# The last sequence's up products as seven block products (Strassen's identity) in an attention and gated-product kernel

## Chip, cores and metric

The kernel runs on one core of a Trainium2 chip. The metric is the device time of one execution in microseconds (us), the median of several runs. Engine names in profile rows: PE is TensorE (PEld its weight loads), DVE is VectorE, ACT is ScalarE, POOL is GpSimd, SP is the engine whose queue issues nearly all DMAs.

## What is computed

```python
def _attn_ref(q, k, v):                 # 4 sequences, 8 heads, 768 tokens, 64 wide
    k_sum = k.reshape(B, H, nb, 32, D).max(axis=3)
    v_sum = v.reshape(B, H, nb, 32, D).mean(axis=3)
    scores_l = scale * q @ k.T          # only where |i - j| < 16
    scores_s = scale * q @ k_sum.T + log(32)
    a = softmax(concatenate([scores_l (masked), scores_s]))
    return a @ concatenate([v, v_sum])

x = attn_out.transpose(0, 2, 1, 3).reshape(3072, 512)
a = x @ w_a                             # 512 x 1536
b = x @ w_b                             # 512 x 1536
return (a * b) @ w_out                  # 1536 x 512
```

## The kernel before

**Precision.** Every large operand is split into a high and a low part that together hold it in float32. A product of two such operands is three matmuls: high by high, high by low, low by high. The float64 weights are brought in as pairs of 32-bit words, joined and split once (`convert`, L451 on), and then stay in SBUF. `weight(f, nm)` is the tile of one block f of 128 of the 1536 columns, nm being a, b or o (w_out).

**Stages.** The tokens are worked in chunks u: the first sequence in three chunks of two tiles of 128 tokens, each further sequence in two chunks of three tiles. Chunks 7 and 8 are the last sequence. An item (u, f) (`item`, L1172) makes, for a chunk of three tiles:
- the up products a and b (`up`, L1151): for each, 4 blocks of the 512 inputs x 3 parts = 12 matmuls of 128x384 into PSUM banks h0 and h1;
- the gate: ACT copies a into g (L1255), DVE multiplies b by g in PSUM (L1258), ACT casts the product to the high part gh (L1260), DVE subtracts for the low part gl (L1263);
- the down products (L1273): for each tile three matmuls of 128x512, summed over the 12 blocks f in banks o0 to o2. After the last f the banks are copied to S1 and stored.

The gate of one item runs while the next item's a is on TensorE. The very last item keeps banks of its own, and its last tile is stored in two halves (L1302 to L1326).

**Attention** of one tile of 128 queries (`scores`, `transposes`, `products`): 16 small matmuls of scores into banks c0 and c1 (L734); for each half of the heads DVE scales and masks (L759) and takes the maximum (L767), ACT makes four exponentials with their sums (L781) and adds 1e-9 (L797), DVE takes the reciprocal (L801), POOL divides (L816); DVE transposes twelve 32x32 patterns over all eight heads (L862, 256 elements per partition); the value products, 16 or 32 small matmuls (L882), go to bank o3. For all tiles but the last of a sequence they are split over two banks: ACT copies one (L904), DVE adds (L907). Then `split` casts the high part (L911) and subtracts for the low part (L915), which are the operands of `up`. The value burst of a tile and the score burst of the next are always issued together. Keys are transposed and their maxima taken once per sequence (L627 to L648); means of values are summed by POOL (L665).

**What sets the order.** Every operation is added to a planner (`Work`) with an engine, a rank, an estimate of its time, and keys that it reads and writes. `emit` picks, engine by engine, the ready operation with the lowest rank; the tables in `ORDER` fix the order by operation number up to about chunk 3. After that the estimates and ranks decide. All engines and SP's queue run what is emitted in order. In the main loop `next(rest)` adds the next tile of attention at chosen items: a chunk's attention is added during the chunk before it, so that attention of chunk 8 runs beside the products of chunk 7.

Of the kernel before, what the change touches and what calls it, by code (L numbers as in the profile page):

```python
# [9 lines left out]
F32 = mybir.dt.float32  # L10
# [20 lines left out]
        547 549 545 558 554 559 555-557 568 564 566 588 567 565 573 585 593 574 594 846 847 854  # L31
        852 853 699 861 859 860 868 866 755 867 873-875 882 880 881 889 809 887 735 888 896 903
        894 895 910 901 902 789 908 909 952 915 917 924 916 843 922 923 929 930 986 987 994 992
        993 995 1002 1000 1001 1027 1028 1003 1066 1008 1009 1067 1074 1072 1073 1075 1082
# [16 lines left out]
        7 3 11 23 15 19 60 59 80 79 72 65 66 73 74 195 67 85-87 196 92 205 93 94 200 201 206 215  # L51
        125 126 216 155 131 156 132 133 138 117 147 139 161 210 162 140 163 236 211 168-170 451
# [6 lines left out]
        441 443 437 643 447 590 572 620 644 592 621 581 645 622 587 623 630 624 631-635 577 636  # L59
        849 637 646-648 851 649 650 856 858 700 702 701 703 754 597 863 716 709 865 870 734 872  # L60
# [3 lines left out]
        954 926 1026 955 845 928 956 962 933 989 969 991 974-982 997 983 984 999 985 1030 1033  # L64
        1034 1032 1005 1035 1036 1007 1106 1042 1049 1069 1054 1055 1071 1056-1064 1077 1065
        1079
# [5 lines left out]
        1229-1232 1234-1237 963 1835 970 1836 1837 1839 1238 1840-1842 1844-1847 1043 1050  # L72
        1849-1853 1856-1858
# [16 lines left out]
    """,  # L90
}

# [1328 lines left out]
```

## Time and profile before

| | us |
|---|---|
| three timed runs | 654.15, 654.19, 654.43 (median 654.19) |
| profiled execution, span from first to last instruction | 652.9 |
| busy: PE, DVE, ACT, POOL | 645.3, 405.3, 255.9, 112.6 |
| DMA | 54.75 MB, mean 84 GB/s |

The profile gives no time of its own for the profiled execution beside the span. The page has these parts: busy time of each engine (1), slices (2), DMA queues (3), the chain of work that ended last, followed back from the end (4), the costliest groups of instructions (5) and DMA issues (6). A matmul's recorded duration overlaps with the next one's; what it costs is seen in the chain in order of time, where a piece lasts until the next begins. PE works at 99% of the span; the other engines are mostly idle, and their idle time costs nothing as long as PE does not wait for them.

### The profile page before, as it was taken

The numbers are of one execution on the slowest core, as the hardware profiler recorded it, in microseconds if no ns is written. First come the engines' busy times: TensorE is split into PE (matmuls) and PEld (weight loads), VectorE is DVE, ScalarE is ACT, GpSimd is POOL, SyncE is SP. The second block draws the span as 40 slices with busy tenths as digits, with TensorE's granted clock in tenths as the row PEclk, the third lists the DMA queues.
The fourth block names the chain that finished last, engine by engine and source line by source line (L and its number), as shares of the span: only waits on it lengthen the run. The fifth ranks groups of instructions, "written<-read, shape, count | busy, mean of one in ns | idle before, by whom it ended". The sixth has DMA issues, their size and how long they took to land.

```text
span 652.9 us, 13600 instructions
## 1 busy us (share of the span) xinstructions
PE 645.3 (99%) x5327; PEld 598.5 (92%) x5327; DVE 405.3 (62%) x830; ACT 255.9 (39%) x750; POOL 112.6 (17%) x202
## 2 busy tenths in 40 slices
PE   8999999999999999999999999999999999999997
PEld 6898888899989999999999999999999999999997
DVE  3789999997785776476646578367456556122212
ACT  3996964523443441333423441144414334121111
POOL 6420030156433431011101100011001011000000
PEclk9999999999999999999999999999999999999999
DMA  9999954554433443421212113132101200010001
GB/s 214 257 230 291 345 141 112 118 122 107 131 80 91 99 96 60 98 49 18 41 27 66 35 34 63 26 94 42 28 14 26 73 10 15 1 49 1 0 1 49
DMA packets 158200, 54.75 MB, mean 84 GB/s; under 512 B 135736, under 2 KB 151352, under 8 KB 158136
## 3 DMA queue, kind: packets, MB, share of 16 engines
q1 hardware_dynamic: 157992, 53.75, 34.5%
q8 instruction: 42, 0.69, 0.4%
q14 instruction: 22, 0.18, 0.1%
q10 hardware_dynamic: 144, 0.13, 0.1%
HBM read 47.41 MB, written 6.44 MB: 82 GB/s over the span
## 4 chain that ended last, share of the span: by engine, by line
PE 95%; ACT 2%; SPq 1%; DMA 1%; issue 1%; DVE 0%; DVEq 0%
PE h L1151 57%; PE o L1273 29%; PE o L882 3%; PE c L734 3%; SPq L353 1%; DMA space<-in_q_dram 1%; PE o L829 1%; PE c L1151 1%; ACT s L781 0%; PE h L1026 0%; PE h L882 0%; PE c L882 0%; PE o L734 0%; PE c L1384 0%; ACT space L781 0%
## 5 line engine op out<-in xcount | busy, mean ns | idle before, releaser
L1151 PE MATMUL h<-x,w 128*128 128x384 f32 (+2 forms) x2064 | 388.3, 321 | 0.1
L1151 PEld LDWEIGHTS h<-x,w 128*128 128x128 f32 x2064 | 331.2, 190 | 10.2 <-issue 0.5
L1273 PE MATMUL o<-w,gh 128*128 128x512 f32 x534 | 131.3, 381 | 0.0
L1260 ACT CAST gh<-h 128x384 fp32r<-128x384 f32 x71 | 33.9, 477 | 207.5 <-DVE h L1258 206.8
L1258 DVE TENSOR_TENSOR h<-h,g 128x384 f32<-128x384 f32 x71 | 40.1, 565 | 115.2 <-PE h L1151 109.7
L862 DVE STREAM_TRANSPOSE pt<-s 32x256 f32<-32x256 f32 x228 | 99.3, 436 | 14.9 <-POOL s L816 10.3
L1273 PEld LDWEIGHTS o<-w,gh 128*128 128x128 f32 x534 | 98.0, 189 | 11.5 <-issue 0.5
L816 POOL TENSOR_TENSOR s<-s,nml 128x480 f32<-128x480 f32 x40 | 43.8, 1096 | 309.9 <-DVE nml L801 309.3
L1151 PE MATMUL h<-late,w 128*128 128x384 f32 x288 | 93.9, 326 | 0.0
L781 ACT ACTIVATE s<-s,nml 128x120 f32<-128x120 f32 x160 | 61.5, 386 | 17.2 <-DVE nml L767 17.1
L1273 PE MATMUL o<-w,gl 128*128 128x512 f32 x231 | 64.0, 384 | 0.0
L1151 PEld LDWEIGHTS h<-late,w 128*128 128x128 f32 x288 | 54.4, 189 | 0.9
L1255 ACT COPY g<-h 128x384 f32<-128x384 f32 x71 | 33.9, 478 | 52.5 <-PE h L1151 52.5
L1263 DVE TENSOR_TENSOR gl<-h,gh 128x384 fp32r<-128x384 f32 x71 | 39.2, 552 | 21.2 <-ACT gh L1260 20.5
L1273 PEld LDWEIGHTS o<-w,gl 128*128 128x128 f32 x231 | 42.9, 189 | 7.2 <-issue 1.6
L665 POOL TENSOR_TENSOR S<-S 96x256 f32<-96x256 f32 (+3 forms) x58 | 33.1, 572 | 45.7 <-DMA S<-in_v_dram 36.3
L781 ACT ACTIVATION_READ_ACCUMULATOR s<-s,nml 128x1 f32 x160 | 30.1, 188 | 0.0
L907 DVE TENSOR_TENSOR o<-o,s 128x512 f32<-128x512 f32 x12 | 8.4, 700 | 32.4 <-ACT s L904 32.2
L759 DVE SCALAR_TENSOR_TENSOR s<-c,mask 128x480 f32<-128x480 f32 x40 | 26.2, 656 | 0.6 <-PE c L734 0.5
L767 DVE TENSOR_REDUCE nml<-s 128x4 f32<-128x480 f32 x40 | 26.1, 653 | 0.7
L1273 PE MATMUL o<-w,x 128*128 128x512 f32 x96 | 25.8, 385 | 0.0
L882 PEld LDWEIGHTS o<-pt,vw 64*64 64x64 f32 (+1 forms) x608 | 19.4, 136 | 5.6 <-issue 5.4
(147 smaller groups left out, 565.7 us busy)
## 6 DMA issues: line engine op xcount, KB each, us to landing
raw<-in_moe_w_a_dram SPq DMA_DIRECT2D x12, 512.0 KB, 6.8
raw<-in_moe_w_out_dram SPq DMA_DIRECT2D x12, 512.0 KB, 6.8
raw<-in_moe_w_b_dram SPq DMA_DIRECT2D x12, 512.0 KB, 7.9
out_dram<-S SPq DMA_DIRECT2D x23, 256.0 KB, 2.2
qin<-in_q_dram SPq DMA_DIRECT2D x288, 16.0 KB, 1.8
S<-in_v_dram SPq DMA_DIRECT2D x24, 192.0 KB, 2.8
kin<-in_k_dram SPq DMA_DIRECT2D x38, 100.0 KB, 2.5
vw<-in_v_dram SPq DMA_DIRECT2D x18, 192.0 KB, 3.2
```

The costliest lines, as they stand in the source:

```text
L665: lambda: nc.gpsimd.tensor_tensor(out=out, in0=i0, in1=i1, op=ALU.add),
L759: lambda h=h: nc.vector.scalar_tensor_tensor(out=s[h], in0=y[h], scalar=0.125, in1=mask[:, kind, None, :KN].broadcast_to([P, NP, KN]), op0 ...
L781: lambda h=h, c=c, sums=sums: nc.scalar.activation(s[h][:, c, :], x[h][:, c, :], AF.Exp, bias=m[:, 0, h, c : c + 1], scale=1.0, accum_out= ...
L816: lambda h=h, r=r: nc.gpsimd.tensor_tensor(out=s[h], in0=s[h], in1=r[:, :, None].broadcast_to([P, NP, KN]), op=ALU.mult,),
L862: lambda js=js, qs=qs, rs=rs: nc.vector.transpose(out=pv[js, rs, qs], in_=sv[qs, rs, js]),
L882: nc.tensor.matmul(bank[dst].rearrange("p (c x) -> p c x", x=P)[h * D : (h + 1) * D, c, es], vw[e][ks_, 2 * c + h, :], d[ks_, h, c, es], s ...
L1151: nc.tensor.matmul(ps, w[:, c, part, :], (xt[:, 4 * xpart : 4 * xpart + 4] if both else inputs_of(u, xpart))[:, :, c].rearrange("p g (a b) ...
L1255: act(CHAIN, 0.13 + W / 1030, [ak], gk, lambda: nc.scalar.copy(out=g, in_=pa))
L1258: lambda: nc.vector.tensor_tensor(out=pb, in0=pb, in1=g, op=ALU.mult),
L1260: act(CHAIN, 0.16 + W / 1030, [bk], [ghk], lambda: nc.scalar.copy(out=gh, in_=pb))
L1263: lambda: nc.vector.tensor_tensor(out=gl, in0=pb, in1=gh.bitcast(F32), op=ALU.subtract),
L1273: nc.tensor.matmul(bank[ok[j]], (gh if first else gl)[:, j * P : (j + 1) * P], w[:, :, part, :].rearrange("p (z a) n -> p z n a", a=2), st ...
```

## The change

**Seven products.** For the last sequence (chunks 7 and 8 together, `whole`) the operands are cut in two: the tokens into halves A1 and A2 (three tiles each), the 512 inputs into halves of 256, and the 256 output columns of one f into a and b. Up products a and b of both halves are then eight block products, each of six matmuls of 128x384. The Winograd form of Strassen's identity makes them from seven products of sums of blocks. With S1 = A21 + A22, S2 = S1 - A11, S3 = A11 - A21, S4 = A12 - S2 and T1 to T4 the like sums of weight blocks: P1 = A11 B11, P2 = A12 B21, P3 = S4 B22, P4 = A22 T4, P5 = S1 T1, P6 = S2 T2, P7 = S3 T3. Their outputs are added on DVE (`sum_`, from PSUM) and POOL (`sum_sb`, in SBUF), five sums on DVE, two on POOL and two gates of 384 columns per f (`step`).

**Sums of weights.** `mixtures(f)` makes T1 to T4 on POOL in float32 from the split weights (2 sums of 128x512, 4 of 128x256), splits them (ACT cast, POOL subtraction, 4 each) and stores them in DRAM (`comb`), with the three plain blocks that are needed, seven stores of 256 KB for each f. They are added at the items of `MIX`, in chunks 3 to 6, outside of the numbered order (`work.aside`). In the last stage `fetch` brings the seven blocks of each f back into a ring of eight places.

**Attention ahead, unrounded.** Chunk 6's products are needed at once and those of the last sequence before `whole`, so attention of chunks 6 to 8 runs earlier (`PLACES`: chunks 3 to 6 hold what 3 to 7 held). From chunk 6 on the result is kept in float32 (`kept`): chunk 6 and 7 through DRAM (`rawd`), chunk 8 in SBUF; the high and low parts are made later (`bring_back`, `inputs_`). The value products of these tiles go to one bank. From chunk 5 on each transposition is cut in two, over four heads each (`SPLIT`). The means of values of the last sequence are summed one sequence earlier.

**Down.** Tiles 0 to 3 of the six are summed over f in o0 to o3 as before. The gated parts of tiles 4 and 5 are kept in SBUF for all f, and their down products run at the end, tile 5 in two halves of 256 columns. Index shifts in `ORDER` and the removed special case of the last item are left out below.

```diff
+    WHOLE, RAW, SPLIT = NU - 2, NU - 3, 5
+    HT = 3 * P
...
+    comb = [dram.tile([8, P, 512], F32, tag=f"comb{f}", name=f"comb{f}") for f in range(NF)]
+    rawd = dram.tile([3 * WIDE, P, 512], F32, tag="raw", name="rawd")
...
-        halves = [slice(0, 4), slice(4, 8)] if False else [slice(0, 8)]
+        halves = [slice(0, 4), slice(4, 8)] if u >= SPLIT else [slice(0, 8)]
...
+        if u >= RAW:
+            other = None
...
-        return dk[0] + dk[1] + vk, [bk] + [other] * bool(other), fn, split
+        return dk[0] + dk[1] + vk, [bk] + [other] * bool(other), fn, kept if u >= RAW else split
...
-    items += [(0, NF - 1), (1, NF - 1)] + [(u, f) for u in range(2, NU) for f in range(NF)]
+    items += [(0, NF - 1), (1, NF - 1)] + [(u, f) for u in range(2, WHOLE) for f in range(NF)]
...
+    PLACES = {(3, 3): 1, (3, 6): 1, (4, 3): 1, (4, 6): 1, (4, 9): 1, (5, 0): 3, (6, 2): 9}
+    MIXED = [(3, 1), (3, 4), (4, 0), (4, 2), (4, 4), (4, 6), (5, 0), (5, 2), (5, 4), (6, 0), (6, 2), (6, 4)]
...
+    def mixtures(f):
...
+        for i, nm in enumerate("ab"):
+            pool(
+                60, 1.3, weight_key(f, nm), [RK[i], f"go{f}"],
+                lambda i=i, nm=nm: nc.gpsimd.tensor_tensor(
+                    out=r[i].rearrange("p h c x -> p (h c) x"), in0=weight(f, nm)[:, :, 0].bitcast(F32),
+                    in1=weight(f, nm)[:, :, 1].bitcast(F32), op=ALU.add,
+                ),
+            )
...
+            act(59, 0.36, [RK[i]], key, lambda: nc.scalar.copy(out=w(0), in_=x()))
+            pool(
+                59, 0.72, [RK[i]], key,
+                lambda: nc.gpsimd.tensor_tensor(
+                    out=w(1), in0=x(), in1=w(0).bitcast(F32), op=ALU.subtract
+                ),
+            )
+            move(
+                99.5, 262.0, 400, key, [f"comb{f}.{op}"], lambda: comb[f][op],
+                lambda: own().bitcast(F32),
+            )
...
+        PROD = {
+            1: ("first", 0, B11), 5: ("s1", 0, T1), 6: ("s2", 0, T2), 3: ("s4", 0, B22),
+            2: ("first", 2, B21), 7: ("s3", 0, T3), 4: ("a22", 0, T4),
+        }
+        TURN = {1: 0.0, 5: 0.1, 6: 0.3, 3: 0.4, 2: 0.5, 7: 0.6, 4: 1.2}
+        FETCH = (1, 5, 6, 3, 2, 7, 4)
+        def bank_of(n, k):
+            return ("h0", "h1", "c0", "c1")[(7 * n + FETCH.index(k)) % 4]
...
+        def step(n):
+            bk = {k: bank_of(n, k) for k in PROD}
+            fetch(n)
+            product(n, 1)
+            copy(bk[1], "p1")
+            product(n, 5)
+            copy(bk[5], "p5")
+            product(n, 6)
+            sum_("u2", bk[6], "p1")
+            sum_sb("c12", "u2", "p5")
+            product(n, 3)
+            sum_("c12", bk[3], "c12")
+            product(n, 2)
+            sum_(None, bk[2], "p1")
+            gate(n, 0, bk[2], "c12")
+            product(n, 7)
+            sum_("u3", bk[7], "u2")
+            sum_sb("c22", "u3", "p5")
+            product(n, 4)
+            sum_(None, bk[4], "u3")
+            gate(n, 1, bk[4], "c22")
...
-        if u is not None and FILL < u < NU - 1 and f in ((3, 7, 11) if u % 2 == 0 else (3, 6)):
-            next(rest)
+        for _ in range(PLACES.get((u, f), 0)):
+            next(rest, None)
+        if (u, f) == (5, 1):
+            bring_back()
+        if u is not None and u > FILL:
+            work.aside = True
+            for g in MIX.get((u, f), ()):
+                mixtures(g)
+            work.aside = False
```

**TensorE in the last stage.** Names: h_77, h_78, c_79, c_80 are the banks h0, h1, c0, c1; o_73 to o_76 are o0 to o3; w_ and gW_ behind the arrow are tiles in the place of former weights. Before, two items of chunk 8 (L1151 is up, L1273 down):

```order
L1151 MATMUL h_78<-x,w_1001 128x384 x12
L1151 MATMUL h_77<-x,w_1031 128x384 x12
L1273 MATMUL o_73<-w_1031,gh 128x512 x2
L1273 MATMUL o_74<-w_1031,gh 128x512 x2
L1273 MATMUL o_75<-w_1031,gh 128x512 x2
L1273 MATMUL o_73<-w_1031,gl 128x512
L1273 MATMUL o_74<-w_1031,gl 128x512
L1273 MATMUL o_75<-w_1031,gl 128x512
L1151 MATMUL h_78<-x,w_1052 128x384 x12
```

Now the middle of a step (L1527 is a product, L1639 a down matmul): three down matmuls of tile 3, P5, P4 of the step before, P6 (its six rows differ in the part of S2), down matmuls of tiles 0 and 1.

```order
L1639 MATMUL o_76<-w_762,w_1300 128x512 x3
L1527 MATMUL h_78<-w_728,w_1181 128x384 x6
L1527 MATMUL c_80<-w_1014,w_1065 128x384 x6
L1527 MATMUL c_79<-w_762,w_1181 128x384
L1527 MATMUL c_79<-w_899,w_1181 128x384
L1527 MATMUL c_79<-w_762,w_1181 128x384 x2
L1527 MATMUL c_79<-w_899,w_1181 128x384
L1527 MATMUL c_79<-w_762,w_1181 128x384
L1639 MATMUL o_73<-w_899,gW_0_6202 128x512 x3
L1639 MATMUL o_74<-w_899,gW_0_6202 128x512 x2
```

A step then goes on with P2, P3, four down matmuls, P7, P1 of the next step and three down matmuls. The four banks go round: each product takes the bank of the fourth product before it in the order 1, 5, 6, 3, 2, 7, 4.

**VectorE in one tile of attention.** Before, a tile of the last sequence, from the query transposition (L1095) over reciprocals (L801) and transpositions (L862) to the second gate product (L1258, with L1263 the low part):

```order
L1095 STREAM_TRANSPOSE qT<-qin 128x512
L1263 TENSOR_TENSOR gl<-h_78,gh 128x384
L801 RECIPROCAL nml_171<-nml_171 128x4 x2
L862 STREAM_TRANSPOSE pt<-s 32x8x32
L1258 TENSOR_TENSOR h_78<-h_78,g 128x384
L862 STREAM_TRANSPOSE pt<-s 32x8x32 x2
L1263 TENSOR_TENSOR gl<-h_78,gh 128x384
L862 STREAM_TRANSPOSE pt<-s 32x8x32 x9
```

Now the last tile of the last sequence (L765 and L773 scale and take maxima, L1278 and L1283 are the gate product and the low part, L807 the reciprocal, L868 a half transposition):

```order
L765 SCALAR_TENSOR_TENSOR s<-c_80,mask 128x4x120
L1278 TENSOR_TENSOR h_78<-h_78,g 128x384
L773 TENSOR_REDUCE nml_172<-s 128x4
L1283 TENSOR_TENSOR gl<-h_78,gh 128x384
L807 RECIPROCAL nml_172<-nml_172 128x4
L868 STREAM_TRANSPOSE pt<-s 32x4x32 x3
L807 RECIPROCAL nml_172<-nml_172 128x4
L868 STREAM_TRANSPOSE pt<-s 32x4x32 x5
L1278 TENSOR_TENSOR h_78<-h_78,g 128x384
L868 STREAM_TRANSPOSE pt<-s 32x4x32 x3
L1283 TENSOR_TENSOR gl<-h_78,gh 128x384
L868 STREAM_TRANSPOSE pt<-s 32x4x32 x13
```

The 24 half transpositions stand where 12 stood, and the first of them no longer stand behind the second half's division.

**POOL beside attention.** Before, the last sums of values (L665, L690) and key maxima (L568) come ahead of the third sequence's tiles, and then the divisions (L816), two for each tile, follow each other with nothing between:

```order
L665 TENSOR_TENSOR S_178<-S_178 96x64
L665 TENSOR_TENSOR vm<-vm,S_178 96x64
L690 TENSOR_SCALAR vm<-vm 96x64
L568 COPY kT<-ksum 128x6x24 x3
L816 TENSOR_TENSOR s<-s,nml_171 128x4x120 x2
L816 TENSOR_TENSOR s<-s,nml_172 128x4x120 x2
```

Now, in chunk 6, sums (L1352), differences (L1392) and splits (L1377) of the mixtures stand around the divisions (L822):

```order
L1377 TENSOR_TENSOR S_191<-S_191 128x2x128
L1392 TENSOR_TENSOR S_191<-S_191 128x256
L822 TENSOR_TENSOR s<-s,nml_171 128x4x120 x2
L1377 TENSOR_TENSOR late<-S_191,late 128x2x128
L1352 TENSOR_TENSOR S_191<-w_1359 128x512
L1352 TENSOR_TENSOR S_191<-w_1430 128x512
L1392 TENSOR_TENSOR S_191<-S_191 128x256
L1377 TENSOR_TENSOR S_191<-S_191 128x2x128
L1392 TENSOR_TENSOR S_191<-S_191 128x256 x2
L1377 TENSOR_TENSOR late<-S_191,late 128x2x128
```

Eight to ten operations of a mixture now stand between the divisions of one tile and of the next.

## Rows read from the trace of the kernel before

**Rows 1.** The page, parts 1 and 4.

```profile
PE 645.3 (99%) x5327; PEld 598.5 (92%) x5327; DVE 405.3 (62%) x830; ACT 255.9 (39%) x750; POOL 112.6 (17%) x202
...
PE 95%; ACT 2%; SPq 1%; DMA 1%; issue 1%; DVE 0%; DVEq 0%
```

**Rows 2.** The chain in order of time: start us, us until the next, what.

```profile
48.10 5.36 PE h L1151 x48
...
244.15 3.90 PE h L1151 x24
248.05 1.94 PE o L1273 x9
249.99 3.90 PE h L1151 x24
...
269.47 1.08 PE o L882 x32
270.55 0.98 PE c L734 x32
```

**Rows 3.** Busy us by stretch: PE, PEld, DVE, ACT, POOL, granted clock, DMA share, GB/s.

```profile
540.00:600.00 60.00, 60.00 (x366) 57.29 (x365) 19.32 (x39) 14.31 (x41) 1.97 (x2) 1.00 0.05 15
```

**Rows 4.** Groups by line and shape: count, busy us, mean ns, idle before, releasers.

```profile
L1258 DVE TENSOR_TENSOR h<-h,g 128x384 f32<-128x384 f32 x71 | 40.1, 565 | 115.2 <-PE h L1151 109.7 <-ACT s L781 3.5 <-ACT nml L797 1.2
L1260 ACT CAST gh<-h 128x384 fp32r<-128x384 f32 x71 | 33.9, 477 | 207.5 <-DVE h L1258 206.8
L759 DVE SCALAR_TENSOR_TENSOR s<-c,mask 128x480 f32<-128x480 f32 x40 | 26.2, 656 | 0.6 <-PE c L734 0.5
L767 DVE TENSOR_REDUCE nml<-s 128x4 f32<-128x480 f32 x40 | 26.1, 653 | 0.7
L665 POOL TENSOR_TENSOR S<-S 96x256 f32<-96x256 f32 x20 | 14.6, 728 | 34.0 <-DMA S<-in_v_dram 32.4 <-DVE half L639 1.2
L1095 DVE STREAM_TRANSPOSE qT<-qin 128x512 f32<-128x512 f32 x20 | 14.1, 707 | 0.0
L907 DVE TENSOR_TENSOR o<-o,s 128x512 f32<-128x512 f32 x12 | 8.4, 700 | 32.4 <-ACT s L904 32.2
L447 POOL TENSOR_TENSOR w<-space,w 128x512 fp32r<-128x512 f32 x6 | 7.9, 1325 | 16.4 <-ACT w L443 16.4
L627 DVE STREAM_TRANSPOSE kT<-kin 128x576 f32<-128x576 f32 x10 | 7.8, 779 | 0.8 <-DMA kin<-in_k_dram 0.7
L627 DVE STREAM_TRANSPOSE kT<-kin 128x192 f32<-128x192 f32 x10 | 3.6, 358 | 0.0
L627 DVE STREAM_TRANSPOSE kT<-kin 128x32 f32<-128x32 f32 x10 | 1.7, 174 | 0.0
```

**Rows 5.** The page, parts 2 (GB/s in 40 slices of the span) and 6.

```profile
GB/s 214 257 230 291 345 141 112 118 122 107 131 80 91 99 96 60 98 49 18 41 27 66 35 34 63 26 94 42 28 14 26 73 10 15 1 49 1 0 1 49
...
out_dram<-S SPq DMA_DIRECT2D x23, 256.0 KB, 2.2
```

**Rows 6.** Timelines of TensorE, VectorE and POOL for one tile: start us, us, what.

```profile
423.52 1.05 PE L734 MATMUL c<-kT,qT 64*64 64x120 f32 x32
...
424.86 0.65 DVE L759 SCALAR_TENSOR_TENSOR s<-c,mask 128x480 f32<-128x480 f32 x1
...
430.52 0.99 POOL L816 TENSOR_TENSOR s<-s,nml 128x480 f32<-128x480 f32 x1 [10.70 <-DVE nml L801]
...
434.49 1.78 DVE L862 STREAM_TRANSPOSE pt<-s 32x256 f32<-32x256 f32 x4 [1.10 <-POOL s L816]
...
438.60 2.71 DVE L862 STREAM_TRANSPOSE pt<-s 32x256 f32<-32x256 f32 x6
```

**Rows 7.** Timelines of POOL and VectorE around one division in the weight conversion.

```profile
91.08 3.52 POOL L816 TENSOR_TENSOR s<-s,nml 128x480 f32<-128x480 f32 x1 [3.56 <-DVE nml L801]
...
91.36 1.20 DVE L495 SCALAR_TENSOR_TENSOR space<-space 128x1024 int32<-128x1024 int32 x1
92.49 1.26 DVE L495 SCALAR_TENSOR_TENSOR S<-S 128x512 int32<-128x512 int32 x2
```

More of the change, by code (lines that the diff above doesn't have):

```diff
@@ L107, in __init__ @@
         self.ops, self.last, self.users, self.free = [], {}, {}, free
-        self.order = {}
+        self.order, self.aside, self.count, self.extra = {}, False, 0, 20000
         for engine, text in ORDER.items():
@@ L117, in add @@
             engine=engine, rank=rank, takes=takes, then=then, rate=rate, fn=fn, left=0,
-            est=0.0, next=[], index=len(self.ops),
+            est=0.0, next=[], index=self.extra if self.aside else self.count,
         )
+        if self.aside:
+            self.extra += 1
+        else:
+            self.count += 1
         need = []
@@ L886, in fn, with kept @@
                             )
+        def kept():
+            if u > WHOLE:
+                halved(t - chunks[u][1], ps)
+                return
+            raw, key = slot("S1", 3)
+            act(
+                CHAIN, 0.6, [bk], [key],
+                lambda: nc.scalar.copy(
+                    out=raw.rearrange("p (c a b) -> p c a b", c=NP, a=2),
+                    in_=ps.rearrange("p c (b a) -> p c a b", a=2),
+                ),
+            )
+            i = 3 * (u - RAW) + t - chunks[u][1]
+            load(80, 262.0, 200, [key], [f"raw.{i}"], rawd[i], raw)
         def split():
@@ L927, in attention_moe @@
     VK = [f"v{i}" for i in range(5)]
-    VS = [f"vs.{h}" for h in range(2)]
     s0 = [sbuf[:, h] for h in range(2)]
@@ L1082, in bring @@
                     load(
-                        97, 49.2, 60, VS, [VK[3 + e]], vbuf[e][r0 : r0 + NS],
+                        97, 49.2, 60, [f"vs{b}.{h}" for h in range(2)], [VK[3 + e]], vbuf[e][r0 : r0 + NS],
                         sums[b].rearrange("h n d -> n h d"),
@@ L1241, in item @@
             pa, pb, g, gh, gl = bank["h0"][:, :W], bank["h1"][:, :W], gt[:, :W], ght[:, :W], glt[:, :W]
-            gk, ak, bk, end = ["g0", "g1"], "h0", "h1", n == total - 1
-            if end:
-                ak, bk, ghk, glk = "c1", "c0", "X6", "X7"
-                pa, pb = bank[ak][:, :W], bank[bk][:, :W]
-                gh, gl = (xt[:, i].rearrange("p c x -> p (c x)")[:, :W] for i in (6, 7))
-                g, gk = slot("S1", 3)
-                g, gk = g[:, :W], [gk]
+            gk, ak, bk = ["g0", "g1"], "h0", "h1"
             for nm, ps, hk in (("a", pa, ak), ("b", pb, bk)):
                 pe(
-                    n - (1.55 if end and nm == "a" else 0) + 0.05 * (nm == "b"), 12 * 0.163, xk + weight_key(f, nm), [hk],
+                    n + 0.05 * (nm == "b"), 12 * 0.163, xk + weight_key(f, nm), [hk],
                     lambda nm=nm, ps=ps: up(nm, f, u, ps),
@@ L1269, in down @@
             w = weight(f, "o")
-            closing = [NF - 1 - (u == NU - 1 and j == m - 1) for j in range(m)]
             for j in banks:
@@ L1275, in down @@
                         w[:, :, part, :].rearrange("p (z a) n -> p z n a", a=2),
[L1276 removed]
+                        start=(f == 0 and first and part == 0), stop=(f == NF - 1 and not first),
                     )
[L1279 to L1331 removed]
@@ L1355, in item, with move @@
                 load(90, 262.0, 200, [key], (), out[row : row + P, :], ob)
+    B11, B21, B12, B22, T2, T4, T1, T3 = range(8)
+    PLACES = {(3, 3): 1, (3, 6): 1, (4, 3): 1, (4, 6): 1, (4, 9): 1, (5, 0): 3, (6, 2): 9}
+    MIXED = [(3, 1), (3, 4), (4, 0), (4, 2), (4, 4), (4, 6), (5, 0), (5, 2), (5, 4), (6, 0), (6, 2), (6, 4)]
+    MIX = {x: (f,) for f, x in enumerate(MIXED)}
+    def move(rank, kb, rate, reads, writes, out, in_):
+        work.add(
+            "SP", rank, 0.45, kb, reads, writes,
+            lambda: nc.sync.dma_start(out=out(), in_=in_()), rate=rate,
+        )
@@ new lines, in bring_back, with parts_ @@
+    def bring_back():
+        for i in range(WIDE):
+            hi, lo = xt[:, i], xt[:, 3 + i]
+            move(
+                85, 262.0, 400, [f"raw.{i}"], [f"X{3 + i}"],
+                lambda lo=lo: lo.rearrange("p c x -> p (c x)").bitcast(F32), lambda i=i: rawd[i],
+            )
+            parts_(
+                30, lambda lo=lo: lo.bitcast(F32), lambda hi=hi: hi, lambda lo=lo: lo, f"X{3 + i}", f"X{i}",
+                f"X{3 + i}", 4 * P,
+            )
+    def parts_(rank, x, hi, lo, xk, hk, lk, n):
+        act(rank, 0.1 + n / 1030, [xk], [hk], lambda: nc.scalar.copy(out=hi(), in_=x()))
+        dve(
+            rank, 0.1 + n / 1000, [xk, hk], [lk],
+            lambda: nc.vector.tensor_tensor(out=lo(), in0=x(), in1=hi().bitcast(F32), op=ALU.subtract),
+        )
@@ new lines, in attention_moe, with space, claim, unrounded @@
+    spare = {}
+    def space(tag, kind):
+        if (tag, kind) not in spare:
+            spare[tag, kind] = wp.tile(
+                [P, 1024], F32 if kind == "in" else F32R, tag=tag, name=f"{kind}{tag.replace('.', '_')}"
+            )
+        return spare[tag, kind]
+    SPACES = ("W0.0", "W0.1", "W1.1", "W2.0")
+    def claim(f, nm, *new):
+        work.add("-", 0, 0, 0, (), weight_key(f, nm) + list(new), lambda: None)
+    def unrounded(i):
+        return space(SPACES[i // 2], "in")[:, i % 2 * 512 : i % 2 * 512 + 512].rearrange("p (c x) -> p c x", c=NP)
@@ L1380, in attention_moe @@
             next(rest)
-    for bk, n in SPIN:
+    whole()
+    for i, (bk, n) in enumerate(SPIN):
         pe(
@@ L1388, in attention_moe @@
         )
+        work.ops[-1].index = 9982 + i
     work.emit()
```

315 lines of the change are left out of this document (252 added, 63 removed), and 39 rows, old and new, of the table ORDER.

## The prediction

> **What bounds the kernel now.** I read the page first, then the chain that ended last, then the queues of one attention tile. The page has TensorE busy for 645.3 of 652.9 us and gives it 95% of the chain [rows 1]. A busy TensorE could still wait inside, so I took its prices from the chain in order of time [rows 2]: 24 up matmuls of 384 columns take 3.90 us (0.1625 each) and nine down matmuls of 512 columns 1.94 us (0.2165 each). One item is then 5.84 us, and the next item in these rows begins 5.84 us later: nothing is waited for. A value burst takes 1.08 us and a score burst 0.98 us. So this kernel's time is the sum of its matmuls, and a change pays by the columns that it removes, less every wait that it brings in. In the last stretch VectorE is busy 19.3 of 60 us, at a granted clock of 1.00 [rows 3]: the attention is over there, and the other engines have room.
>
> **What goes.** The last sequence needs eight block products for each f before, now seven; each is six matmuls of 384 columns. 6 x 12 = 72 matmuls fewer, 72 x 0.1625 = **11.70 us** of TensorE, all of it on the path. The down matmuls keep their columns, but the last tile is now computed in halves: 72 of 256 columns at 5.36/48 = 0.112 us [rows 2] against 36 of 512 at 0.2165 add 8.04 - 7.79 = **0.24 us**. The value products that went to two banks go to one; the bursts cost the same, so that gives TensorE nothing, and VectorE is spared a sum of 0.70 us [rows 4] for each such tile. The end keeps its form: a last 256-column product, one copy, a DMA.
>
> **The last stage, one step** (first order excerpt). Seven products at 0.975 and twelve down matmuls are 6.83 + 2.60 = 9.42 us. Counting from the start of P5: P4 of the step before ends at 1.95, P6 at 2.93, P2 at 4.98, P3 at 5.96, P7 at 7.80, P1 of the next step at 8.77. VectorE does nine operations at 0.565 [rows 4], 5.1 us of 9.4. With about 0.1 us from TensorE to its reader and ScalarE's 0.48 between them, the low part of P4 is done at 4.4, and P3 wants its bank at 4.98; the low part of P2 is done at 9.1, and the next P5 wants its bank at 9.42. POOL's sum of 384 columns lies between its 0.73 for 256 and 1.33 for 512 [rows 4], say 1.0, against 2.2 us of room. So I price the chain at **nothing**, under a cover of 0.3 us; a chain that ran 0.8 us longer would cost 12 x 0.5 = 6 us, and that is my upper bound.
>
> The products' weights come by DMA: 84 loads of 262 kB in 113 us, 195 GB/s. The trace has 256 KB landing 2.2 us after its issue, and a stretch at 345 GB/s [rows 5]; eight places in the ring let several be in flight, so I count the loads as hidden. [...] No row here shows small loads that follow each other so closely for so long, so this stays a rival, below.
>
> **The mixtures** are 12 x 10 POOL operations. Two sums of 512 columns at 1.33 and eight of 256 at 0.73 make 8.5 us for each f [rows 4], 102 us in the 280 us of chunks 3 to 6, where POOL now does little but divisions of 0.99 [rows 6]. None adds a column to TensorE, but they stand in POOL's queue among the divisions (third excerpt), with ScalarE's casts that they wait for and 84 stores on SP's queue. What waits behind a late sum is a division, then 12 transpositions, then the value burst on TensorE.
>
> **Attention ahead** is the main term that I take off the gain. The tiles of chunks 7 and 8 now run by the end of chunk 6, and the value bursts stand closer to their scores. Between the end of a tile's scores and its value burst, the order of the change leaves these matmuls, at the prices above: 17.55, 16.9, twice 15.6, 14.95, 14.3, and five times 13.65 us (60 up and 18 down, or 48 and 27), apart from the two long ones in which keys are prepared. Before it was 16.25 to 23.4.
>
> What has to fit is seen in one tile [rows 6]: the score burst ends at 424.50, the first scaling starts at 424.86, and the last transposition ends at 441.31, 16.8 us after the burst. That would not fit into 13.65. The change splits the transpositions in halves, so that the first twelve start after the first division. A half has 128 elements; on VectorE a transposition took 0.78 us for 576, 0.36 for 192 and 0.17 for 32 [rows 4], so 0.147 + 0.0011 an element, 0.29 for a half, 0.30 with the gap to the next. It can be no less than half of the present 0.445 (0.22) and no more than the 0.36. I take 0.30, which lies on the line through three shapes: 24 x 0.30 = 7.2 us.
>
> The tile of the second excerpt then runs so: scaling from 0.15; two pairs of scaling and maximum, 1.3 us each, a gate product, the query transposition (0.71) and a low part, to 4.5; a reciprocal to 4.7; the division to 5.7; then 24 halves, two more gate operations and a reciprocal, 7.2 + 1.2 + 0.2 with gaps, to **14.4**. The matmuls end at 13.65: TensorE waits 0.75 us. The same sum on the other tight tiles: 0.35 and 0.4 where the gate product falls later; 0.9 and 0.8 for the last two, where sums and splits of the new halves (0.4 to 0.7 each, an estimate from the 0.565 for 384 columns) stand ahead of the next scaling; 1.0 in the window of 14.3, which still has the sum from two banks and a split in front; 0.3 in that of 14.95; 0.1 in the wider ones. Together **4.6 us**. At 0.22 a half nothing would wait; at 0.36 each of nine tiles would wait 1.4 us more, 13 us in all.
>
> **Contention.** One division took 3.52 us instead of 0.99, beside three VectorE operations that each read two SBUF operands [rows 7]. The change adds 33 such operations (the sums and splits of the halves, some 15 us) to the stretch where POOL is busy; those of the last stage read PSUM. Nothing is lost if they miss the divisions, and 2.5 us each time that one is stretched as in the row, three times at most, for the three tiles beside which they lie: 0 to 7.5. I take **0.6**, near the low end, since the new operations are a third as long as those of the row. [...]
>
> **Sum.** 652.9 - 11.70 + 0.24 + 4.6 + 0.6 = 646.6 for the span. The three timed runs, 654.15 to 654.43, are some 1.3 us over the profile's span; that is what lies around it, so **647.9** against 654.19. Below some 0.2% (1.3 us) a measurement of this kernel can't tell a change from none.
>
> **The rivals.**
> 1. No wait shows: halves cheaper than 0.25 us and divisions on time, 654.19 - 11.46 = 642.7. For it: VectorE is idle for several us in the tile of [rows 6], which the halves may fill. Against: the windows are up to 10 us shorter than before. 12%.
> 2. Slower, by POOL: a mixture sum of 1.33 stands in front of a division or between the two of a tile, and the cast or the store that it needs is late. Place: chunks 4 to 6. Price: a sum and a difference, 2.0 us, less the 0.4 that the waits above cover already, for 12 tiles, 19 us, and 667. It decides against the change once the twelve tiles wait 0.95 us each. For: the third excerpt has mixtures right before and right behind the divisions. Against: mixtures fill 36% of POOL's time there. 10%.
> 3. The last stage is bound by its chain or by its loads: 2 to 6 us on top, 650 to 654. Loads one after another, at 2.2 us each [rows 5], would need 185 us for a stage of 113; under 184 GB/s the gain is gone. Against: the 345 GB/s of the same rows. 10%.
> 4. VectorE is held by POOL, as POOL by VectorE in [rows 7]: of the 33 operations 36% meet one of POOL's and wait for half of it, 0.43 us on average: 5 us more, 652.8. Against: the VectorE operations of these rows kept their pace. 6%.
>
> That the products are not removed is excluded: the order of the change has 504 of their matmuls where 576 stood.
>
> **How the numbers follow.** My forecast, waits of 2 to 9 us and so 644.5 to 651.5, has 62%. Faster by over 0.2%: 0.62 + 0.12, and 0.11 for the milder two thirds of rivals 3 and 4: 0.85. Same 0.06, slower 0.09. The range takes in rival 1 and the milder half of 3: 643.0 to 652.5; what is left out, rival 2 and the strong forms of 3 and 4, is some 19%.
>
> **What would show it.** Right: TensorE idles in short pieces before the value bursts of chunks 5 and 6, with VectorE's transpositions named as the releaser, some 5 us together; half transpositions at 0.29 us; steps of 9.4 us in the last stage without a wait. Wrong: steps of over 9.8 us, with TensorE waiting for a low part or a DMA; value bursts that wait for divisions behind mixtures; or no idle time at all.

## The result, and the profile after

The changed kernel takes **661.2 us** (median, 661.07 to 661.37) where the kernel before takes 654.31 (654.15 to 655.3) on the same chip: a ratio of 1.0096, 95% interval 1.0081 to 1.0111. It is slower by 1%, where 647.9, 1% faster, was forecast. Its profiled execution has a span of 659.5 us, 12.9 more than the 646.6 of the sum.

The page of the changed kernel, parts 1 and 4 (before: [rows 1]):

```profile
PE 641.8 (97%) x5064; PEld 591.3 (90%) x5064; DVE 467.0 (71%) x1050; ACT 275.5 (42%) x812; POOL 235.9 (36%) x346
...
PE 71%; DVE 15%; SPq 5%; ACT 4%; issue 2%; DMA 2%; POOL 1%; ACTq 0%; DVEq 0%
PE h L1178 29%; PE o L1292 15%; DVE pt L868 10%; PE c L1527 6%; PE h L1527 6%; PE o L1639 5%; SPq L359 4%; PE o L890 3%; PE c L740 2%; PE h L1639 2%; DVE h L1278 2%; ACT s L787 1%; DVE gl L1283 1%; DMA comb<-S 1%; DMA space<-in_q_dram 1%
```

TensorE had 95% of the chain and now has 71%. A quarter of it has gone to others: VectorE's transpositions (L868) 10%, SP's issuing of loads (L359) 4%. The part to be read is the one in which the chain leaves TensorE.

**The last stage is as forecast.** The chain in order of time (start us, us, what): the same five down matmuls in three steps that follow each other:

```profile
555.31 1.08 PE o L1639 x5
564.73 1.08 PE o L1639 x5
574.14 1.08 PE o L1639 x5
```

A step takes 9.41 us, 9.42 was worked out, and in this stretch the chain never leaves TensorE.

**Chunks 3 to 6 are not.** The chain of the worst place, around 426 us (SPq is SP's queue issuing DMAs):

```profile
421.19 1.76 SPq L359
...
423.04 2.16 DMA comb<-late
425.30 0.07 ACT late L1374
...
425.61 0.48 ACT gh L1280
426.14 4.21 PE o L1292 x9
430.34 4.21 PE h L1178 x24
```

The timelines of SP, of ScalarE and of TensorE there (start us, us, what, and in brackets the idle time before it and what ended it):

```profile
413.29 9.65 SPq L359 DMA_DIRECT2D qin<-in_q_dram  x16
423.04 0.38 SPq L1336 DMA_DIRECT2D comb<-late  x1
```
```profile
414.92 0.48 ACT L1275 COPY g<-h 128x384 f32<-128x384 f32 x1 [0.19 <-PE h L1178]
425.30 0.40 ACT L1374 CAST late<-S 128x256 fp32r<-128x256 f32 x1 [9.90 <-DMA comb<-late]
425.61 0.47 ACT L1280 CAST gh<-h 128x384 fp32r<-128x384 f32 x1
```
```profile
426.14 2.93 PE L1292 MATMUL o<-w,gh 128*128 128x512 f32 x6 [4.44 <-ACT gh L1280]
```

Read upwards: the down matmuls wait for the gate's cast (L1280). That cast stands in ScalarE's queue behind the cast of the next mixture (L1374), which has waited 9.90 us for the DMA that empties its staging buffer. The store was issued only at 423.04, since 16 loads of queries stood ahead of it on SP and took 9.65 us to issue. TensorE stands still for 4.4 us, and what follows is slow: nine down matmuls take 4.21 us and 24 up matmuls 4.21, where [rows 2] have 1.94 and 3.90. The granted clock says why: it is at 0.50 there (stretch, PE, PEld, DVE, ACT, POOL busy, granted clock, DMA share, GB/s):

```profile
422.00:424.00 2.00, 0.00 (x0) 0.00 (x0) 0.00 (x0) 0.00 (x0) 0.00 (x0) 0.99 0.11 22
424.00:426.00 2.00, 0.00 (x0) 0.00 (x0) 0.00 (x0) 0.70 (x3) 0.22 (x1) 0.50 1.01 290
426.00:428.00 2.00, 1.86 (x4) 1.51 (x5) 1.85 (x4) 0.61 (x3) 0.50 (x1) 0.50 0.70 195
...
430.00:432.00 2.00, 2.00 (x11) 1.91 (x11) 0.88 (x4) 0.57 (x4) 0.99 (x1) 0.80 0.16 25
432.00:434.00 2.00, 2.00 (x14) 2.00 (x13) 0.06 (x1) 1.34 (x6) 0.00 (x0) 1.00 0.21 33
```

A second kind of wait is short and frequent. The chain around 326 us:

```profile
324.74 0.31 DVE pt L868
...
325.08 0.58 DVE h L1278
...
325.68 0.49 ACT gh L1280
...
326.21 1.56 PE o L1292 x6
```

The gate's product (L1278) stands in VectorE's order among halved transpositions, and the down matmuls wait until it has had its turn. Groups of VectorE by line and shape (count, busy us, mean ns, idle before, releasers):

```profile
L868 DVE STREAM_TRANSPOSE pt<-s 32x128 f32<-32x128 f32 x288 | 87.2, 303 | 13.5 <-POOL s L822 8.6
L868 DVE STREAM_TRANSPOSE pt<-s 32x256 f32<-32x256 f32 x84 | 36.6, 436 | 2.4 <-PE o L890 0.6 <-POOL s L822 0.4
L1278 DVE TENSOR_TENSOR h<-h,g 128x384 f32<-128x384 f32 x48 | 27.0, 563 | 21.4 <-PE h L1178 19.5 <-ACT nml L803 1.2
```

A half costs 0.303 us, near the forecast (0.29), but two halves are 0.606 where a whole one is 0.436: over 144 pairs 24 us more of VectorE. The line through the two leaves 0.17 us for an instruction without elements, an estimate from these two rows.

**The account.** I took the time from each matmul's start to the next one's, less the usual interval of that shape, and kept the pieces over 0.25 us between 280 and 520 us:

| what TensorE waited for | us | priced at |
|---|---|---|
| the late store: 4.6 at 426 (4.4 of it idle), 1.0 at 400, slow matmuls behind the first 2.6 | 8.2 | 0 |
| gates: 2.2 behind halved transpositions, 0.7 behind the preparation of keys, 0.4 behind exponentials | 3.3 | 0 |
| inside value bursts, for transpositions, 7 times | 4.0 | 4.6 |
| divisions on POOL that VectorE holds | none | 0.6 |

That is 15.5 against 5.2, so 10.3 of the 12.9 us. A further 0.7 are the value bursts of seven tiles, which take 1.08 us each in one bank where they took 0.98 in two; the rest is in smaller pieces.

POOL and VectorE did get in each other's way, though not at a division: beside the mixtures none took over 1.00 us. The timelines of POOL and VectorE where they met, and of VectorE where POOL was idle (the mixtures are L1392 and L1377, the low parts that read two operands from SBUF L1414), and VectorE's group (ns: least, median, most):

```profile
362.79 0.73 POOL L1392 TENSOR_TENSOR S<-S 128x256 f32<-128x256 f32 x1
363.07 1.00 DVE L1414 TENSOR_TENSOR x<-x 128x512 fp32r<-128x512 f32 x1
...
493.73 2.05 POOL L1392 TENSOR_TENSOR S<-S 128x256 f32<-128x256 f32 x2
494.50 0.69 DVE L1414 TENSOR_TENSOR late<-inW,x 128x512 fp32r<-128x512 f32 x1
495.11 2.83 DVE L1414 TENSOR_TENSOR w<-inW,w 128x256 fp32r<-128x256 f32 x5
...
515.28 1.76 DVE L1414 TENSOR_TENSOR w<-inW,w 128x256 fp32r<-128x256 f32 x5
```
```profile
L1414 DVE TENSOR_TENSOR w<-inW,w x15: 409/417/949, 495.1 to 521.3; 128x256 fp32r<-128x256 f32 x15
```

The 128x512 operation takes 1.00 us beside POOL's, 0.69 alone (at 419.66 us). The five at 495.11 take 2.83 us; five such operations take 1.76 at 515.28, where POOL is idle. Two of the first five took 0.95 and 0.94 us instead of 0.42, and the second POOL operation at 493.73 takes 1.24 instead of 0.73, as it started 0.04 us behind VectorE's. So three of the 33 new VectorE operations were held, 1.4 us in all. Two of them stand in the chain in front of the exponentials for which a gate waits 0.4 us; how much of that is theirs, no run separates.

### The profile page after: what moved, and what is told of

It reads as the page before. It is cut to its first block, busy times and chain, and to the rows that moved or that the text cites. A ratio compares the mean times of both kernels' runs of the same rounds, so it can differ in the third digit from the quotient of the medians.

```text
span 659.5 us, 13990 instructions
## 1 busy us (share of the span) xinstructions
PE 641.8 (97%) x5064; PEld 591.3 (90%) x5064; DVE 467.0 (71%) x1050; ACT 275.5 (42%) x812; POOL 235.9 (36%) x346
## 4 chain that ended last, share of the span: by engine, by line
PE 71%; DVE 15%; SPq 5%; ACT 4%; issue 2%; DMA 2%; POOL 1%; ACTq 0%; DVEq 0%
PE h L1178 29%; PE o L1292 15%; DVE pt L868 10%; PE c L1527 6%; PE h L1527 6%; PE o L1639 5%; SPq L359 4%; PE o L890 3%; PE c L740 2%; PE h L1639 2%; DVE h L1278 2%; ACT s L787 1%; DVE gl L1283 1%; DMA comb<-S 1%; DMA space<-in_q_dram 1%
## 5 line engine op out<-in xcount | busy, mean ns | idle before, releaser
L1178 PE MATMUL h<-x,w 128*128 128x384 f32 (+2 forms) x1608 | 295.7, 320 | 0.1
L1178 PEld LDWEIGHTS h<-x,w 128*128 128x128 f32 x1608 | 253.8, 190 | 9.8 <-issue 1.0
L868 DVE STREAM_TRANSPOSE pt<-s 32x128 f32<-32x128 f32 (+1 forms) x372 | 123.8, 333 | 15.9 <-POOL s L822 9.0
L1292 PE MATMUL o<-w,gh 128*128 128x512 f32 x396 | 100.1, 389 | 7.7 <-ACT gh L1280 7.6
L822 POOL TENSOR_TENSOR s<-s,nml 128x480 f32<-128x480 f32 x40 | 43.8, 1096 | 149.6 <-DVE nml L807 148.3
L1178 PE MATMUL h<-late,w 128*128 128x384 f32 x192 | 62.8, 327 | 0.0
L1280 ACT CAST gh<-h 128x384 fp32r<-128x384 f32 x48 | 22.9, 476 | 90.9 <-DVE h L1278 90.9
L1278 DVE TENSOR_TENSOR h<-h,g 128x384 f32<-128x384 f32 x48 | 27.0, 563 | 21.4 <-PE h L1178 19.5
L1392 POOL TENSOR_TENSOR S<-S 128x256 f32<-128x256 f32 x48 | 35.6, 741 | 1.9
L1283 DVE TENSOR_TENSOR gl<-h,gh 128x384 fp32r<-128x384 f32 x48 | 26.4, 550 | 13.7 <-ACT gh L1280 13.0
L1527 PE MATMUL c<-w,w 128*128 128x384 f32 x180 | 33.8, 326 | 0.0
L1527 PE MATMUL h<-w,w 128*128 128x384 f32 x180 | 33.7, 326 | 0.0
L1352 POOL TENSOR_TENSOR S<-w 128x512 f32<-128x512 f32 x24 | 30.3, 1276 | 7.4 <-DMA out_dram<-S 6.9
L1527 PEld LDWEIGHTS c<-w,w 128*128 128x128 f32 x180 | 30.3, 189 | 0.7
```

What stands on the lines that cost most here:

```text
L822: lambda h=h, r=r: nc.gpsimd.tensor_tensor(out=s[h], in0=s[h], in1=r[:, :, None].broadcast_to([P, NP, KN]), op=ALU.mult,),
L868: lambda js=js, qs=qs, rs=rs: nc.vector.transpose(out=pv[js, rs, qs], in_=sv[qs, rs, js]),
L1178: nc.tensor.matmul(ps, w[:, c, part, :], (xt[:, 4 * xpart : 4 * xpart + 4] if both else inputs_of(u, xpart))[:, :, c].rearrange("p g (a b) ...
L1278: lambda: nc.vector.tensor_tensor(out=pb, in0=pb, in1=g, op=ALU.mult),
L1283: lambda: nc.vector.tensor_tensor(out=gl, in0=pb, in1=gh.bitcast(F32), op=ALU.subtract),
L1292: nc.tensor.matmul(bank[ok[j]], (gh if first else gl)[:, j * P : (j + 1) * P], w[:, :, part, :].rearrange("p (z a) n -> p z n a", a=2), st ...
```

## The experiments

Three theories. **A**: the place of the mixtures' stores on SP, which reaches TensorE through ScalarE's queue. **D**: the halved transpositions hold the gates and the value products (from the second set of runs on D', sharper: what they add to VectorE's load is what makes it late). **P**: the mixtures' time on POOL itself. A ratio is always to the kernel before, with its 95% interval. Where an edit changes a rank or an instruction, the planner also puts other operations in another order, and what is measured is both together.

### The stores first, and the planner's estimate

```diff
-                99.5, 262.0, 400, key, [f"comb{f}.{op}"], lambda: comb[f][op],
+                60, 262.0, 400, key, [f"comb{f}.{op}"], lambda: comb[f][op],
```

> The stores of the mixtures get rank 60 in place of 99.5, so that SP takes them ahead of the loads of queries and values (97, 98); nothing else is edited. Theory A (a store stands on SP behind 16 query loads, ScalarE's next cast of a mixture waits for the store to free the staging buffer, and the gate's cast waits behind it): the 4.4 us pause of TensorE at 426 us, the slow matmuls behind it (2.4 us) and the wait at 400 us (0.9 us) go: 661.2 - 7.7 = 653.5, between 651.5 and 655. Theory D (the halved transpositions on VectorE hold the gates and the value products): the stores don't matter, 660 to 661.5. Theory P (the mixtures' work on GpSimd holds the divisions or VectorE): 660 to 662.

Measured: 656.24 us, ratio 1.0019 (1.0009 to 1.0028), 5 us less than the change. The timelines of SP and ScalarE at the same place of this run:

```profile
411.28 0.38 SPq L1336 DMA_DIRECT2D comb<-late  x1
...
413.56 7.43 SPq L359 DMA_DIRECT2D qin<-in_q_dram  x16
```
```profile
421.23 0.48 ACT L1280 CAST gh<-h 128x384 fp32r<-128x384 f32 x1 [5.72 <-DVE h L1278]
```

The store goes out ahead of the 16 loads, no cast waits, and the gate's cast starts as soon as VectorE has the product. Both pauses are gone. So A is real, but of its 8 us only 5 come back: the value bursts wait some 1.5 us more than they did and the gates 1.1, presumably since VectorE had used the pauses to catch up.

```diff
-                        rank + 0.02 * n, 0.05 + 0.4 / len(halves), sk[n:] if n else sk[: 2 // len(halves)] + ["S0.2"] * own, [f"{key}{i}{j}"],
+                        rank + 0.02 * n, 0.317 if len(halves) == 2 else 0.45, sk[n:] if n else sk[: 2 // len(halves)] + ["S0.2"] * own, [f"{key}{i}{j}"],
```

> The planner is told 0.317 us for a halved transposition (what one takes from start to start in the trace) in place of 0.25, so that it puts the gate's operations on VectorE earlier among the transpositions and the value products later; no operation changes. Theory D: the waits of down products for a gate that stands behind transpositions (0.85, 0.34, 0.60, 0.71, 0.44 and 0.41 us) go, and part of the 4.5 us inside value bursts: 656 to 658.5. Theory A: the store and its pause stay, so not below 655; by A alone 660 to 662. Theory P: 660 to 662.

> Both edits, the stores' rank and the estimate of the halved transposition. If A and D both hold and add up: 661.2 - 7.7 - 4 = 649.5, between 647.5 and 652, which is faster than the kernel before (654.3). A alone: 653.5. D alone: 657. P: 660 to 662.

Measured: 660.75 us, ratio 1.0092 (1.0076 to 1.0107), for the estimate alone; with the stores first 662.81, 1.0117 (1.01 to 1.0135), slower than the stores alone. The first is outside D's range; it lies where A or P alone had put it, but not for A's reason. The second is outside every range. With the estimate alone, the waits for gates and for late stores do fall, from 8.9 us to 2.6, the pause at 426 among them. But the halves then end later, and TensorE waits 3.0 us inside the last value burst and 6.3 behind it, where the last stage begins, at a mean granted clock of 0.74 from 510 to 530 us. With the stores first as well, TensorE waits 3.0 and 6.3 us at the same places, and 2.3 at 370: a store had come behind 16 loads there all the same, and ScalarE's cast waited 6.5 us for it. The chain of the run with the estimate alone:

```profile
518.23 0.32 DVE pt L868
...
518.59 1.30 PE o L890 x26
...
519.91 0.60 ACT inW L1443
...
525.72 0.35 DVE w L1414
526.07 0.04 issue
526.11 1.97 PE h L1527 x5
```

The last value burst is followed by VectorE's sums for the last stage, and TensorE waits for them until 526. VectorE has as much to do as in the change; what has moved is the place where it is late.

### No sums; casts on POOL

> The sums of weights are left out: their stores carry plain blocks of the weights (as many stores, of the same size), so GpSimd's 102 us of mixtures, ScalarE's 48 casts and the staging buffers have no part in it, and the last sequence's output is that of other weights. Theory A: nobody waits for a store any more, 653 (651.5 to 655), like the stores put first. Theory P: the divisions come free of the mixtures as well, 647 to 651. Theory D: 660 to 661.5.

Measured: 653.88 us, ratio 0.9982 (0.9972 to 0.9993). That is what A asks for, and 2.4 us below the run with the stores first, which speaks for a little of P. But the planner lays out everything anew when so much is missing, so the second reading is weak.

```diff
-            act(59, 0.36, [RK[i]], key, lambda: nc.scalar.copy(out=w(0), in_=x()))
+            pool(59, 0.6, [RK[i]], key, lambda: nc.gpsimd.tensor_copy(out=w(0), in_=x()))
```

> The stores stay behind the loads, but the 48 rounding copies of the mixtures are made by GpSimd instead of ScalarE, so that a late store holds GpSimd and no gate. Theory A (the harm is done by ScalarE's queue): the pause at 426 us goes, 654 to 657, as with the stores first. If the harm of a late store reaches TensorE through GpSimd's divisions as well: 658 to 664.

Measured: 655.72 us, ratio 1.0014 (1.0003 to 1.0024). The stores still stand behind the loads, and POOL now waits for them (the waits of POOL: in total, times, longest):

```profile
POOL late L1374 <- DMA comb<-late: 25.3, 6, 8.5
```

The pauses at 400 and 426 us are gone, and TensorE loses no more than with the stores first. So a late store was dear because the cast that waits for it stood in the queue of the gates. (The edit also takes the time of 48 casts off ScalarE, which this run does not separate.)

### The transpositions whole

```diff
-    WHOLE, RAW, SPLIT = NU - 2, NU - 3, 5
+    WHOLE, RAW, SPLIT = NU - 2, NU - 3, 99
```

> Only the halving of the transpositions is undone (SPLIT 99 in place of 5): 12 of 0.436 us in place of 24 of 0.303 us per tile of the last four chunks' attention, 24 us of VectorE less. The stores stay behind the loads. Theory D' (VectorE, 82 to 90% busy between 330 and 520 us, is what holds gates and value bursts; the stores' rank adds its own pause): gate waits (3.4 us) and value waits (3.9 us) fall by half or more, the store's pause stays or moves: 656 to 659. Theory A alone: 660 to 662. A rival, that the halves are what lets the transpositions start 1.1 us earlier, behind the first division, and so what keeps the value bursts in time: 662 to 665.

> Whole transpositions and the stores ahead of the loads. Theory D' with A: 656.2 of the run with the stores first, less half or more of its 7 to 8 us of gate and value waits: 649 to 653, faster than the kernel before. If the halves keep the value bursts in time: 656 to 660.

Measured: 654.6 us, ratio 0.9993 (0.9981 to 1.0005), and with the stores first 653.17, 0.9969 (0.9956 to 0.9982). The first is faster than D' had it (656 to 659), the second just above its range (649 to 653). The halving, which was to make the attention fit, cost more than the late stores. VectorE's load (behind the length of the stretch, PE and PEld) in the change, then in the run with whole transpositions and the stores first:

```profile
300.00:330.00 30.00, 29.14 (x331) 26.58 (x330) 21.48 (x59) 11.78 (x38) 17.45 (x22) 1.00 0.49 151
330.00:360.00 30.00, 29.39 (x218) 27.78 (x217) 25.30 (x68) 15.13 (x53) 11.46 (x14) 1.00 0.51 146
360.00:390.00 30.00, 29.01 (x213) 26.71 (x212) 25.76 (x72) 11.59 (x36) 17.30 (x21) 1.00 0.58 161
```
```profile
330.00:360.00 30.00, 30.00 (x224) 28.53 (x223) 21.20 (x45) 15.36 (x54) 9.75 (x13) 1.00 0.48 136
360.00:390.00 30.00, 30.00 (x223) 28.39 (x222) 23.23 (x54) 11.24 (x37) 17.29 (x22) 1.00 0.64 166
```

From 330 to 390 us VectorE is busy for 84 to 86% in the change, and TensorE waits; with whole transpositions it is 71 to 77%, and TensorE is busy throughout. The load is not all: from 300 to 330 us the change has VectorE at 72%, and TensorE waits there too, for the gates behind halves at 306 and 326. These two runs show what the halving costs, not how that divides between VectorE's load and the places in its order. Most of the waits that are left in the second run lie in front of the last stage (a gate waits 1.2 us at 465). Its chain:

```profile
513.54 0.99 PE h L1527 x6
...
515.71 1.34 DVE w L1414 x4
517.05 0.35 DVE inW L1492
...
518.76 0.35 DVE w L1414
...
519.15 1.88 PE h L1527 x5
```

TensorE has two pauses of 3.4 and 0.8 us, for sums of the last three tiles (L1492) and their low parts (L1414), which VectorE makes for the second tile only after the last transposition.

### The seam on POOL: faster than both kernels

For the first two of the three tiles the sums and low parts go to POOL:

```diff
+                side, eng, slow = (pool, nc.gpsimd, 0.74) if i < 2 else (dve, nc.vector, 0.36)
...
-                    dve(
-                        rank + 0.01 * j, 0.36, ks_, [ko],
+                    side(
+                        rank + 0.01 * j, slow, ks_, [ko],
```

> The run with whole transpositions and the stores first, and in it the sums of the first two of the last three token tiles (4 sums and 5 low parts each, 18 operations of 0.43 to 0.49 us) move from VectorE to GpSimd, which has little to do then. Theory S (what is left in that run is the seam in front of the last stage: product 5 waits 3.4 us, and 0.8 us again, for sums that VectorE makes only behind the last transpositions, and the clock falls to 0.91 there): both pauses and the slow matmuls go, 653.2 - 5.5 = 647.7, between 646 and 650. Rival: GpSimd at 0.74 us for an operation, or the rounding copies on ScalarE, are as late: 651 to 655.

> As the run with the seam on GpSimd, and the 48 rounding copies of the mixtures on GpSimd too, so that ScalarE waits for no store at all. Theory A (the 1.2 us pause at 465 us, exponentials and a gate behind a cast that waits for a store, is the last of the stores' harm): 1 to 2 us less than the run without, 646.5 (644.5 to 649). If GpSimd, with 20 us more and the seam's sums, holds the divisions: 649 to 654.

Measured: **648.46 us, ratio 0.9900 (0.9884 to 0.9917)**, as theory S had it, and with the casts on POOL as well 649.34, 0.9916 (0.9893 to 0.9939), which is the same: the 1 to 2 us expected of it did not come. The first is 1% faster than the kernel before. That it lies 0.6 us from the forecast for the change confirms nothing of that forecast, as it is another kernel. The pauses at the seam are not gone but shrink from 3.4 and 0.8 us to 1.2 and 0.6, and the granted clock stays at 1.00. VectorE in front of the seam has 19.94 us of work in 30 where the run without this edit has 23.66:

```profile
480.00:510.00 30.00, 30.00 (x225) 28.51 (x223) 19.94 (x44) 13.10 (x48) 13.21 (x17) 1.00 0.40 122
```
```profile
480.00:510.00 30.00, 30.00 (x225) 28.53 (x224) 23.66 (x52) 13.11 (x48) 5.18 (x5) 1.00 0.40 119
```

### Each cost put back alone

The fastest version with one edit undone, or with the sums taken out:

> The fastest version so far (whole transpositions, stores first, seam on GpSimd: 648.5), with the stores' rank back at 99.5, behind the loads. If the three costs add up, the late stores bring their 5.0 us back: 653.5 (652 to 655). If they cost only what they did among whole transpositions (1.4 us between the two runs with them): 649.5 to 651.

> The fastest version so far with the transpositions halved again (SPLIT 5). Theory D' (24 us more of VectorE in the stretch where it is over 80% busy make gates and value bursts late): 654 to 657, as the run with the stores first, whose seam did not pause. Rival, that the halves cost only where they push work into the seam, which GpSimd has taken over here: 649 to 651.

> The fastest version so far with the sums of weights left out (stores carry plain blocks, the last sequence's output is that of other weights): GpSimd loses about 100 us of work and ScalarE 48 casts. If the mixtures as such cost TensorE nothing once stores and VectorE are mended, as the prediction had it: 648 to 649. If they still hold divisions or exponentials, as the 2.4 us between the run without sums and the one with the stores first say: 645.5 to 647.

| put back | us | ratio (95%) | cost |
|---|---|---|---|
| stores behind the loads | 650.18 | 0.9928 (0.9913 to 0.9943) | 1.8 us |
| halved transpositions | 655.63 | 1.0012 (1.0001 to 1.0023) | 7.3 us |
| the seam on VectorE (the run above) | 653.17 | 0.9969 (0.9956 to 0.9982) | 4.5 us |

(The cost is the difference of the ratios times 654.9 us; that of the stores is barely larger than its uncertainty.) The costs don't add up: among whole transpositions a late store hurts less (in this pair TensorE has the same order in both). The halved transpositions cost what D' said. Without the sums 652.82 us came out, 0.9974 (0.9954 to 0.9995), slower than with them and outside both ranges. The new plan has a wait of 1.9 us for a gate at 398 us and pauses of 0.9 and 1.9 us at the seam. Leaving work out is no measurement of it where a planner answers with another order.

So the last question was put with the order kept. POOL's operations stay where they are, but the sums and differences work on 4 columns in 128:

```diff
-                    out=r[x[0]][:, x[1]], in0=r[y[0]][:, y[1]], in1=r[z[0]][:, z[1]], op=op
+                    out=r[x[0]][:, x[1], :, :4], in0=r[y[0]][:, y[1], :, :4], in1=r[z[0]][:, z[1], :, :4], op=op
```

> The fastest version so far (648.5), every instruction at its place, but GpSimd's sums and differences of weights (72 of its 120 operations for the mixtures, 66 of 101 us) work on 4 columns of every 128, so that most of their time is gone; what they leave out makes the last sequence's output another. If the mixtures' time costs TensorE nothing by itself: 648 to 649. If it does (2.4 us for all of it, by the pair with halved transpositions): 646.3 to 647.5.

> The same in the changed kernel as it is (661.2): order kept, 66 us of GpSimd's sums gone, the same part of the output another. If the mixtures' time costs nothing by itself, and only the place of their stores and the transpositions do: 660 to 661.5. If it is GpSimd's time that makes stores and divisions late: 656 to 659.

Measured: in the fastest version 649.25 us, 0.9912 (0.9892 to 0.9932), no gain: there the mixtures' time costs nothing that can be measured (by the two intervals at most some 1 us). In the change as it is 658.11, 1.0053 (1.0031 to 1.0075), 2.8 us less than with full sums and in the range of P. In that run's trace TensorE stands still for 2.9 us before the gate at 425 us where it was 4.4; the other waits are much as they were. So in the change P is worth some 3 us, and what its trace shows of that works through A.

## Why the prediction was wrong

**What held.** 72 matmuls fewer, at their prices: the last stage runs in steps of 9.41 us (9.42 worked out), without a wait, so rival 3 falls. Its 84 loads, which land 3.0 us after their issue, were hidden: the page's slices from 528 to 626 us have 194 to 250 GB/s, with these loads in pieces of 256 KB. A halved transposition takes 0.303 us (0.29), and 0.317 from start to start (0.30). The value bursts waited 4.0 us (4.6), 0.3 to 0.8 in each of seven tiles.

So all three signs that were to show the forecast right came out, and the time was 13 us off: none of them looks at the gates or at ScalarE's queue.

**What held in kind and not in size: contention.** No division beside the mixtures was held (none took over 1.00 us), so the 0.6 were not needed. The trace shows VectorE held, beside POOL's differences and splits: 0.42 us became 0.95 and 0.94, and 0.69 became 1.00. Rival 4 named that and put it at some 12 of the 33 operations and 5 us; it was three, and 1.4 us of VectorE.

**What failed, by the steps of the prediction.**

1. *The mixtures: "None adds a column to TensorE".* I listed the queues in which they stand, and then followed only one of them, POOL's, to the divisions. The path that hurt was through ScalarE: a store late on SP, a cast that waits for it, a gate behind the cast. Priced at nothing, it lost TensorE 8.2 us in the trace, and mending it gives back 5.0. Rival 2 had the late store, but let it act on divisions and value bursts. The transpositions' waits for divisions are 9.0 us in all, and were 10.3 before; what was to show rival 2 is not there.
2. *"Attention ahead."* The duration of a half was right, and the sum of the waits inside the value bursts was near; the rest of the term was missing. I counted the gate operations as time that VectorE spends in a tile, and not as something that TensorE waits for: 2.2 us behind halves, 3.3 with the others. And I took the halving as a help, from one tile's chain, without adding up VectorE over the stretch: 24 us more, which left it 83 to 91% busy from 330 to 390 and from 450 to 510 us. Put back alone, the halving costs 7.3 us. And the bursts do not "cost the same" in one bank: 0.10 us more in each of seven tiles.
3. *The clock* stood in no term. A pause of 4.4 us cost 2.6 us more in slow matmuls.
4. *The seam* between attention and the last stage was priced as part of a tile's window (0.9 and 0.8 us). In the change itself it is quiet, presumably because the earlier waits let VectorE finish; among whole transpositions it costs 4.5 us. The run with truthful estimates showed it first, with 6.3 us.

What stays open: how the 15.5 us divide between A and D in the change itself, since mending one moves the other's waits; the runs show only what each costs beside the others as they then stood.

## What to carry to other kernels

When work is moved into another engine's shadow, follow every queue in which its pieces stand, and price not the piece but whatever stands behind it there: a store behind 16 loads was dear here because a cast on the engine of the gates waited for it. Add up the busy time of the engine that the moved work leans on over the whole stretch: splitting an instruction to shorten one chain added 24 us to VectorE here and cost 7.3. Where a planner sets the order, mend the durations of things, not the estimates alone, and test a cost with the order kept.

## What the hardware showed that was not expected

- SP needed 9.65 us to issue 16 loads of 16 KB, 0.43 to 0.44 us for 13 of them and 0.73, 0.90 and 1.76 for the others; in the run with the stores first the same 16 took 7.43.
- The granted clock fell to 0.50 while TensorE stood still for 4.4 us at 422 to 426, and was back at 1.00 after 432. It stayed at 1.00 through a pause of 2.3 us at 370 us in the run with both first edits. In the run with whole transpositions and the stores first it stayed at 1.00 through the 3.4 us of the first pause, from 514 to 518, and fell behind it (0.82 in 518 to 520, 0.50 in 520 to 522), with TensorE at work again from 519.
- VectorE was held by POOL and POOL by VectorE: at 495.11 us VectorE's 0.42 us became 0.95 beside a POOL operation that ran already, and at 494.54 POOL's 0.73 became 1.24 behind a VectorE operation that had started 0.04 us earlier.
